# Turning the attention weights on TensorE in fp32, in the bank of their scores, and a list schedule for the issue order

## The chip, the core and the metric

The kernel runs on one core of a Trainium2 chip. The core has five instruction queues: PE (TensorE, matrix products), DVE (VectorE), ACT (ScalarE), POOL (GpSimd) and SP (SyncE, which only issues transfers here). ACT issues transfers as well. Each queue works strictly in its own order and waits for others by semaphores. The metric is the time of one execution in microseconds (us).

## The reference, cut to what matters

```python
# q, k, v: 4 batches x 8 heads x 576 tokens x 64, float32
scores = scale * q @ k.T                       # 576 x 576 for each of 32 heads
thresh = max(scores, -1) - tau
scores = where(scores >= thresh, scores, -1e9)
attn = exp(scores - max); attn = attn / (sum(attn) + 1e-9)
x = attn @ v                                   # put together: 2304 tokens x 512
# two blocks of products on x
h = ((x @ w1) * (x @ w2)) @ w3 @ w_out
out = elu(h @ w_in) @ w_out2
```

## The kernel before

The program has an attention phase and then products in sequence. Only the phase is changed.

**Tiles.** The 32 heads go as 16 pairs. The scores of a pair are cut into 9 tiles of 128 queries by 576 keys, 144 tiles in all. The tiles of the first four pairs (NPL = 4, 36 tiles) multiply queries and keys in plain fp32 and are called plain tiles here. The others use queries and keys that were split into a high and a low part in fp32r. A tile passes through these steps, each an operation of its own:

- `emit_S` (PE, L367 for plain tiles, L379 for the others) writes the scores into `s`, which takes two banks of PSUM. There are three such buffers, so six of the eight banks.
- `emit_max` (DVE, L388) takes the row maximum into `st`. `emit_tiny` (DVE, L392) makes the threshold and the bias of the exponential from it.
- `emit_exp` (ACT, L396) writes `e` in SBUF. `emit_mask` (DVE, L402) sets what lies under the threshold to zero and sums the rows. This is the last reader of `s`.
- `emit_H` (ACT, L409) rounds `e` to fp16 and `emit_L` (POOL, L413 and L414) makes the fp16 rest. Both lie in `hl`.
- `emit_T` (SP, L424, L426, L429) turns `hl` by a transposing transfer into `pt`, the keys on the partitions.

A group is a pair's first four or last five tiles, 256 or 320 tokens. `emit_PV` (PE, L483) multiplies a group's `pt` with the values `v` in fp16, as three partial products (high by high, low by high, high by low): 28 matmuls into 64 rows each. The values were scaled and split before that (`v_sum`, `v_mean`, `v_scale`, `prep_v`, `prep_vl`: ACT, PE, DVE). Row sums go another way: `turn_r` (PE, L443) transposes the 4 or 5 columns of reciprocals, and a store and a load spread them over partitions (`rd`, `rb`). `emit_xf` (DVE, L491) multiplies the two, and `emit_xh`, `emit_xl` split the result into `x`.

**First layers.** `emit_ab` (PE, L525) computes a = x w1 and b = x w2. One unit is 12 matmuls over four pairs of one batch, 256 or 320 tokens wide. The units of three of the four batches belong to the phase and fill PE between tiles; they need the batch's x and the converted weights. `pv`, `ab` and a small filler product (`keep_busy`, L384, during the first 18 tiles) share the two banks that are left.

**Order.** The phase's operations are written down with what each needs, and a table of letters says in which order they are issued. Each queue then holds its instructions in this order. Behind the phase come the last batch's first layers, M = w3 w_out (L828), x2 = g M (L968) and the second layers (L1001, L1030).

Of the kernel before, what the change touches and what calls it, by code (L numbers as in the profile page):

```python
# [7 lines left out]
F32 = mybir.dt.float32  # L8
# [35 lines left out]
PSCALE = 2.0 ** 14
VSCALE = 2.0 ** 15
LNS = 14 * 0.6931471805599453
KINDS = dict(
    a="emit_H",
    b="emit_L",
    c="emit_PV",  # L50
    d="emit_S",
    e="emit_T",
    f="emit_exp",
    g="emit_mask",
    h="emit_max",
    i="emit_rr",
    j="emit_tiny",
    k="emit_xf",
    l="emit_xh",
    m="emit_xl",  # L60
    n="evict_a",
    o="evict_g",
    p="high",
    q="join",
    r="keep_busy",
    s="keep_r",
    t="load_plain",
    u="load_qk",
    v="load_r",
    w="load_v",  # L70
    x="load_w",
    y="low",
    z="prep_h",
    A="prep_lk",
    B="prep_lq",
    C="prep_v",
    D="prep_vl",
    E="rest",
    F="run_ab",
    G="sign",  # L80
    H="store_g",
    I="store_r",
    J="top",
    K="turn_r",
    L="v_mean",
    M="v_scale",
    N="v_sum",
)
# the order in which the operations of the attention phase are issued
ORDER = (  # L90
    "wttdNxwdwhjdfhjgfthtdjgfhadgJbLjhdftEearjMfgbahdCtgbaxjGdeNbhaihfeKrbjjLqrfrerfwggedauDbspxhdMajgyfI",
    "hdCijgrfbrhJdegajEdeNbhaKGLsrfbejrhacqfIbgpegdayMJjDdhNvrifjbheagfbjekdfglxEKLershavdgbaGdCuhbacjjMq",
    "fbfgephdgJIyjhdfmaigKeabhdCjjDsefbhavcgefbDaIdezEbjgfkAdaxhgbejhdafGBejifvgKcbqeaslhbpdekglxmjehdfyk",
    "ajgfhdabmljgrfhbzdgJwjmhdBiaejEKFahfIbeGFfugbjegfdqaAedsngavbhpxdhbacjjhfoyfIjgfegdzkbidhJgrAajhdfeE",
    "blKFjageaGbdsnhfveqcbaNugebpjhdfIkFmehajBjgfxFofgydJgdhndaeizbLhFjjEavbeFhfMaobgefcGabjgnelfqKdbaHFh",
    "seCuBgdpIkdjhmFfiyjofegKFlgsJdhbndDavIobcejhahabfeEFjkfwmgHzvAFeGgnabdjofFqabhdpcjgbfehnaugydeNFkjhf",
    "eidajbgKFslhfImoedlgzLFbjehnfvdjBoeFfMgaAhHCdiHcgnbavhaujbmefDdKgFAejkfwhbdajgaFbhesfojaIgdbenrfhdaF",
    "BjgfhzbudgeFaijbhfvejoKNdgbFsahenfBjLdMHgcfbehaIoeabjdgfFhezAijkfvdgAFnugChbeldoaKrjhsdbefjDaFmgeahl",
    "bfdcnIhBzvgjjbfdeawFgmavkbhfudiFjagbelofhdNAeFjgnfhbHadoezKLjcBMgCehsbfDdeaFkwgbHahedniBFajhfjbfIgKF",
    "ujgmfoedAsndglaembFhazvhbejdjofcbgfuIhaAgdejhdfvBiagNvbhdajeKLcsbMfIjkehabljgfekdabgfehdavbgezidhbre",  # L100
    "ajrhrfbjjKsvgcfumfBgeldkmdgelahmdaIehbFCjjhabeDfFjfgwbngfdcAzvgeoaihadbeNudhFjbhefkajgKBFesfjfgbednL",
    "aIdheFabMglCoHbdjhHfFiajgAenfvmKdhFbegsaIjhfbdeoaDFzjgwnhBfvdocuhbajjgfAagdefFkbagzvdhbdNuhFenibajhf",
    "ejjKLFsBfgIeofgAdnczgehbaiejdkbfFheljauMmgdfvbFoahCgbeadDKndajbhefchsvAejjgffgbdHFzkHgBelhadFawjbhfi",
    "jobdfIgFuheaBgnKdjoselbFhNIfeLAdMngFavejmadfuboFheahCbcgzvjibnjDfdekFfBgvHhadmgFabjlheaKdjsofwbecfgb",
    "nIgezhAdjFehfkadjHofvbFggNdehncailjhbfuemajdkKFgbsaehfdboaeLjFgfhmlIedjabMFgnCeiBdzvoFDfhmKawFAjgfen",
    "dbsvochuaAjeghadbHkfjFlgbefhdzIgFbejnhfdBjoFfgahmudegFabnjhNdboeaFihfjbavHjgKLFsnefbfgdeAcaoaHgbzehd",
    "FMbekjifhBdaIjgFnlhfBejCKdgbFsvmeofhadgeabFnIhujjAfvdofcDbggzvdehFkahaubjdlFfhmniawejbKfFogbejadfchB",
    "HngzebjgdfeFkNgseahIdbLFhelajjMfbodfgFAaignedhbFjoHfeBagdavheAKFahnsjmjHfdbFgobfIhdnvcgbChvjDfdejiaw",
    "ckhbagfKjFksfgeagdlNFemhobjdenlLFaMbhfIejdobFgeihdneaFhfbjmKHfFgsvogHdCFehnaIjjfdbveoaFhbDecnjavgfbf",
    "gFekldFoagHbdcnaeabdeFkibldKeFosImeFmneFovHdFncvoFkldFmnoH",  # L110
)
# [48 lines left out]
def attention_moe_moe2(  # L160
# [56 lines left out]
    def conv_ops(key, parts, eng):  # L217
        """Steps that turn a loaded chunk into the parts (x -> (high, low)) it is used in."""
# [43 lines left out]
    mul2 = cst.tile([P, 2], F32, name="mul2")  # L262
# [14 lines left out]
    def load_plain(p, j, eng=A):  # L277
# [221 lines left out]
    def xl_pool(p, n):  # L499
        return int(n == 1 or p % 2)  # L500
# [610 lines left out]
```

## Time and profile before

| | us |
|---|---|
| time, three runs | 1074.71 (median), 1073.62, 1080.15 |
| span of the profiled execution | 1067.1 |
| median less span | 7.6 |
| PE busy | 970.9 (91%) |
| DVE busy | 644.9 (60%) |
| ACT busy | 519.7 (49%) |
| POOL busy | 484.5 (45%) |

The profile shows one execution; its own time is not listed apart, so its span is set against the median, and 7.6 us are taken as what lies around the span. Start times count from the span's start. PEld is TensorE's weight load, which runs beside PE. A merged row of the timeline gives the start of the first instruction, the time covered and the count; the length of a matmul is that of one alone, longer than the step from one to the next.

### The profile page before, as it was taken

To read this page: it belongs to the slowest core of one execution; us is meant where nothing else is said; L and a number is where in the kernel's file an instruction comes from. 1 tells how busy PE (TensorE), PEld (TensorE's weight loads), DVE (VectorE), ACT (ScalarE), POOL (GpSimd) and SP (SyncE) were. 2 spreads that over 40 slices of the span, in tenths; PEclk is the share of its full clock that TensorE was granted. 3 is DMA by queue.
4 is the path that set the end of the run, shared out by engine and by line. 5 is a ranking of instruction groups with operands and counts; after the bars stand their busy time and mean duration, and the time that the engine had idled before them with its cause. 6 is when DMAs were issued, how large, how long until landed. Compare 5 with 4: busy or idle time off the path is not lost.

```text
span 1067.1 us, 16849 instructions
## 1 busy us (share of the span) xinstructions
PE 970.9 (91%) x6132; PEld 871.6 (82%) x6132; DVE 644.9 (60%) x1200; ACT 519.7 (49%) x870; POOL 484.5 (45%) x494
## 2 busy tenths in 40 slices
PE   7476788878888798889999999999999999999998
PEld 4344677777888788789879999989999999999997
DVE  7799999867888698636564664943332232323322
ACT  5566776756776675525344565433233232322322
POOL 3568888877777675614221232232222222222221
PEclk9879999988999899999999999999999999999999
DMA  8989999999999999977616673300000000000000
GB/s 236 162 176 224 187 182 186 194 180 156 207 208 183 183 161 161 156 184 240 219 58 220 204 243 114 119 1 30 1 1 30 1 30 1 1 30 1 31 1 29
DMA packets 207342, 131.52 MB, mean 123 GB/s; under 512 B 175792, under 2 KB 194460, under 8 KB 202652
## 3 DMA queue, kind: packets, MB, share of 16 engines
q1 hardware_dynamic: 189520, 66.45, 39.1%
q10 hardware_dynamic: 17740, 64.01, 20.2%
q8 instruction: 48, 0.79, 0.3%
q14 instruction: 34, 0.28, 0.1%
HBM read 73.73 MB, written 14.23 MB: 82 GB/s over the span
## 4 chain that ended last, share of the span: by engine, by line
PE 62%; DMA 16%; DVE 15%; ACT 2%; issue 2%; POOL 1%; SPq 1%; ACTq 0%; POOLq 0%; DVEq 0%
PE h L1001 18%; PE o L1030 18%; PE x L968 10%; PE ab L525 9%; DMA pt<-hl 8%; DMA rb<-rd 4%; DVE e L402 4%; PE m L828 4%; DVE st L388 3%; DVE st L392 3%; DMA rqk<-in_qk 2%; PE s L379 1%; PE s L367 1%; DMA rd<-rt 1%; ACT e L396 1%
## 5 line engine op out<-in xcount | busy, mean ns | idle before, releaser
L525 PE MATMUL ab<-x,W 128*128 128x256 f32 (+1 forms) x1536 | 222.2, 299 | 9.7 <-DVE xf L491 5.8
L525 PEld LDWEIGHTS ab<-x,W 128*128 128x128 f32 x1536 | 209.8, 191 | 13.5 <-DVE xf L491 4.5
L413 POOL TENSOR_TENSOR hl<-e,hl 128x512 f16<-128x512 f32 x144 | 171.7, 1192 | 104.3 <-ACT hl L409 90.7
L1001 PE MATMUL h<-sl,W 128*128 128x384 f32 x1152 | 216.5, 336 | 0.0
L1030 PE MATMUL o<-WO,sl 128*128 128x512 f32 x864 | 213.8, 392 | 0.8 <-POOL sl L1022 0.8
L1001 PEld LDWEIGHTS h<-sl,W 128*128 128x128 f32 x1152 | 203.7, 188 | 7.7
L1022 POOL TENSOR_TENSOR sl<-th,sl 128x384 fp32r<-128x384 f32 x87 | 88.1, 1013 | 265.7 <-ACT sl L1017 265.7
L1030 PEld LDWEIGHTS o<-WO,sl 128*128 128x128 f32 x864 | 160.9, 188 | 29.4 <-POOL sl L1022 1.2
L1010 DVE TENSOR_SCALAR th<-h 128x384 f32<-128x384 f32 x96 | 53.4, 556 | 182.1 <-PE h L1001 182.1
L396 ACT ACTIVATE e<-s,st,esc 128x576 f32<-128x576 f32 x144 | 117.5, 826 | 72.8 <-DVE st L392 57.5
L1011 ACT ACTIVATE th<-th 128x384 f32<-128x384 f32 x96 | 50.4, 525 | 193.7 <-DVE th L1010 193.7
L402 DVE SCALAR_TENSOR_TENSOR e<-s,st,e 128x576 f32<-128x576 f32 x144 | 115.3, 807 | 18.9 <-ACT e L396 18.4
L379 PE MATMUL s<-qk 128*128 128x288 f32 x480 | 91.1, 320 | 32.4 <-DVE e L402 27.2
L409 ACT ACTIVATE hl<-e 128x576 f16<-128x576 f32 x144 | 94.8, 674 | 35.4 <-DMA pt<-hl 23.1
L388 DVE TENSOR_REDUCE st<-s 128x1 f32<-128x576 f32 x144 | 106.9, 747 | 8.0 <-PE s L379 4.6
L379 PEld LDWEIGHTS s<-qk 128*128 128x128 f32 x480 | 72.8, 201 | 43.2 <-issue 19.4
L968 PE MATMUL x<-sl,M 128*128 128x384 f32 x576 | 101.9, 338 | 0.0
L968 PEld LDWEIGHTS x<-sl,M 128*128 128x128 f32 x576 | 101.5, 187 | 0.3 <-DVE sl L215 0.2
L1015 DVE SCALAR_TENSOR_TENSOR th<-th,h 128x384 f32<-128x384 f32 x96 | 53.2, 554 | 58.2 <-ACT th L1011 57.4
L1017 ACT ACTIVATE sl<-th 128x384 fp32r<-128x384 f32 x96 | 50.3, 524 | 76.9 <-PE o L1030 47.6
L483 PE MATMUL pv<-pt,v 128*64 128x256 f16 (+1 forms) x896 | 66.3, 300 | 13.1 <-DMA pt<-hl 8.2
L392 DVE SCALAR_TENSOR_TENSOR st<-mul,st,add 128x2 f32<-128x2 f32 x144 | 76.5, 541 | 0.8
(86 smaller groups left out, 1033.9 us busy)
## 6 DMA issues: line engine op xcount, KB each, us to landing
rqk<-in_qk ACTq DMA_DIRECT2D x24, 576.0 KB
raw_wo<-in_wo ACTq DMA_DIRECT2D x12, 1024.0 KB
th<-g_dr SPq DMA_DIRECT2D x48, 192.0 KB
raw_w<-in_w ACTq DMA_DIRECT2D x8, 1024.0 KB
raw_w<-in_w3t ACTq DMA_DIRECT2D x8, 1024.0 KB
raw_win<-in_win ACTq DMA_DIRECT2D x8, 1024.0 KB
g_dr<-g SPq DMA_DIRECT2D x16, 320.0 KB
out<-r SPq DMA_DIRECT2D x18, 256.0 KB
```

The costliest lines, as they stand in the source:

```text
L379: T.matmul(s[:, n, :HS], q, k[:, c:c + HS], start=(x == 0), stop=(x == len(ops) - 1))
L388: V.tensor_reduce(st[i][:, 0:1], sc[i][:, :, :HS], axis=AX.XY, op=ALU.max, negate=True)
L392: V.scalar_tensor_tensor(t[:, 1:3], mul2, t[:, 0:1], add2, op0=ALU.mult, op1=ALU.add)
L396: A.activation(et[i], sc[i][:, :, :HS], AF.Exp, bias=st[i][:, 2:3], scale=esc)
L402: V.scalar_tensor_tensor(et[i], sc[i][:, :, :HS], st[i][:, 1:2], et[i], op0=ALU.is_ge, op1=ALU.mult, accum_out=sm[p][:, pos:pos + 1],)
L409: A.activation(hl[i][:, :S], et[i].rearrange("p a b -> p (a b)"), AF.Copy)
L413: G.tensor_tensor(t[:, S + 64:], e[:, :512], t[:, :512], op=ALU.subtract)
L525: T.matmul(o[:, :w], wf[:, m, wx, kt, :], x[:, xx, :], start=(k == 0), stop=(k == 3 * NK - 1))
L968: T.matmul(o[:, :TB], M[:, f, mx, e * P:(e + 1) * P], gh[j, f][:, gx, :], start=(k == 0), stop=(k == 23),)
L1001: T.matmul(o[:, :TB], WI[f][:, wx, kt, :], xh[j, kt][:, xx, :], start=(k == 0), stop=(k == 3 * NK - 1),)
L1022: (V if jobs else G).tensor_tensor(x[:, 1, :], thin[2 + f % 2], f32(x[:, 0, :]), op=ALU.subtract)
L1030: T.matmul(po[j, t], gg[j, f][:, gx, t * P:(t + 1) * P], WO[f // 2][:, f % 2, wx, :], start=(f == 0 and k == 0), stop=(f == NF2 - 1 and k ...
```

## The change

1. The weights of a tile are no longer split and turned by transfer. `emit_X` transposes `e` on PE in five blocks of 128 keys, in fp32, into the banks that held the tile's scores (the fourth and fifth block overlap by 64 keys, and the values of that half block are zero). `emit_C` (ACT) copies the 640 columns to `pt`, now fp32. So a tile's `s` is held until `emit_C` is done. `emit_H`, `emit_L` and `emit_T` are gone.
2. `emit_PV` multiplies `pt` with the values as they are, in fp32: ten matmuls of 64 rows in place of 28, issued as five pieces. The five steps that scaled and split the values are gone.
3. The threshold is made on POOL (`emit_tiny`); the bias of the exponential is the maximum itself, since the queries are scaled once on POOL (`prep_s`); plain tiles make it on POOL (`emit_bias`). `emit_xl` is on POOL always.
4. The loads and stores of the phase that ACT issued are issued by SP.
5. The letter table is replaced by a list schedule that runs while the program is written. Each operation has an engine, a length and a key; at each step the engine that can start first takes, among the operations ready within 0.05 us, the one with the lowest key. Units of `ab` are cut into pieces of three matmuls. A tile's transposes have its number less 2 as key.
6. Buffers: `e` 5 in place of 4, values 4 in place of 1.

```diff
-            SP.dma_start_transpose(pt[g][:, :, j, c:c + P], hl[i])
+    def emit_X(i):
+        e = et[i].rearrange("p a b -> p (a b)")
+        o = sc[i].rearrange("p a b -> p (a b)")
+        for c in range(5):
+            k = min(c * P, S - P)
+            T.transpose(o[:, c * P:(c + 1) * P], e[:, k:k + P], ident)
+
+    def emit_C(i):
...
+        x = sc[i].rearrange("p a b -> p (a b)")[:, :5 * P].rearrange("p (c q) -> p c q", c=5)
...
+            A.activation(pt[g][:, :, j, c:c + P], x, AF.Copy)
-    def emit_PV(p, n):
+    def emit_PV(p, n, c):
...
+        for j in range(2):
+            x_ = q[:, c, j, :w // D if p < NPL else w]
+            T.matmul(
+                po_[p, n][j * D:(j + 1) * D, :w], vt[p][:, j, c * D:(c + 1) * D], x_,
+                start=(c == 0), stop=(c == 4),
+            )
-        V.scalar_tensor_tensor(t[:, 1:3], mul2, t[:, 0:1], add2, op0=ALU.mult, op1=ALU.add)
+        G.tensor_scalar(t[:, 1:2], t[:, 0:1], -1.0, add2[:, (k := int(i >= NPL * TPP)):k + 1], op0=ALU.mult, op1=ALU.add)
-    "wttdNxwdwhjdfhjgfthtdjgfhadgJbLjhdftEearjMfgbahdCtgbaxjGdeNbhaihfeKrbjjLqrfrerfwggedauDbspxhdMajgyfI",
+                t, o = min(((t, o) for t, o in cand if t <= t0 + 0.05), key=lambda x: (x[1].key, place[id(x[1])]))
-        ring["s", i] += [mx, ex, mk]
+        xo = op(call(emit_X, i), [mk], "PE", 0.5, i - 2)
+        co = CC[i] = op(call(emit_C, i), [xo], "ACT", 0.68, i - 3)
+        ring["s", i] += [mx, ex, mk, xo, co]
```

PE's queue around tile 105 in the kernel before (the number behind s or e is the tile; the last number only names the buffer):

```order
L379 MATMUL s105_3953<-qk11_1288 128x288 x4
L525 MATMUL ab1_0_1_1_3962<-x4_0_1782,W1_468 128x256 x3
L525 MATMUL ab1_0_1_1_3962<-x5_0_2296,W1_468 128x256 x3
L525 MATMUL ab1_0_1_1_3962<-x6_0_2639,W1_468 128x256 x3
L525 MATMUL ab1_0_1_1_3962<-x7_0_2938,W1_468 128x256 x3
L379 MATMUL s106_3985<-qk11_1288 128x288 x4
L525 MATMUL ab1_0_2_0_3992<-x4_0_1782,W2_623 128x256 x3
L525 MATMUL ab1_0_2_0_3992<-x5_0_2296,W2_623 128x256 x3
L525 MATMUL ab1_0_2_0_3992<-x6_0_2639,W2_623 128x256 x3
L525 MATMUL ab1_0_2_0_3992<-x7_0_2938,W2_623 128x256 x3
L443 MATMUL s105_3953<-ident_115,rr11_0_3942 4x128
L379 MATMUL s107_4018<-qk10_1071 128x288 x2
```

Here scores and units of `ab` alternate, and a tile stands once in the queue. PE's queue around tile 108 in the changed kernel (L329 scores, L370 transposes, L475 `ab`, L400 `turn_r`):

```order
L329 MATMUL s108_3842<-qk8_740 128x288 x4
L475 MATMUL ab1_0_4_1_3850<-x4_0_1505,W4_723 128x256 x3
L475 MATMUL ab1_0_4_1_3850<-x5_0_1816,W4_723 128x256 x3
L475 MATMUL ab1_0_4_1_3850<-x6_0_2055,W4_723 128x256 x3
L475 MATMUL ab1_0_4_1_3850<-x7_0_2554,W4_723 128x256 x3
L329 MATMUL s109_3869<-qk8_740 128x288 x4
L400 MATMUL s109_3869<-ident_108,rr11_1_3830 5x128
L475 MATMUL ab1_0_5_0_3883<-x4_0_1505,W5_881 128x256 x3
L475 MATMUL ab1_0_5_0_3883<-x5_0_1816,W5_881 128x256 x3
L475 MATMUL ab1_0_5_0_3883<-x6_0_2055,W5_881 128x256 x3
L370 MATMUL s108_3842<-ident_108,e108_3867 128x128 x5
L475 MATMUL ab1_0_5_0_3883<-x7_0_2554,W5_881 128x256 x3
```

A tile now stands twice, with its transposes (which wait for its mask on DVE) ahead of the `ab` piece that needs nothing of it.

PE's queue around tiles 62 to 67 in the changed kernel, behind 16 units of `ab` in a row (64 pieces of 320 columns):

```order
L475 MATMUL ab0_1_7_1_2345<-x3_1_1415,W7_1180 128x320 x3
L370 MATMUL s62_2045<-ident_108,e62_2084 128x128 x5
L370 MATMUL s63_2064<-ident_108,e63_2094 128x128 x5
L370 MATMUL s64_2069<-ident_108,e64_2108 128x128 x5
L400 MATMUL s64_2069<-ident_108,rr6_1_2130 5x128
L329 MATMUL s65_2381<-qk11_1227 128x288 x4
L329 MATMUL s66_2388<-qk11_1227 128x288 x4
L438 MATMUL pv6_1_2398<-pt6_1_1974,vr6_1235 64x320 x2
L329 MATMUL s67_2406<-qk10_1080 128x288 x4
L438 MATMUL pv6_1_2398<-pt6_1_1974,vr6_1235 64x320 x6
L370 MATMUL s65_2381<-ident_108,e65_2404 128x128 x5
L438 MATMUL pv6_1_2398<-pt6_1_1974,vr6_1235 64x320 x2
```

In the kernel before a tile's scores stand between these units; now the scores of tiles 62 to 64 are ahead of the run and their transposes behind it, and no `ab` is left for the tiles that follow.

POOL's queue around tile 108 in the changed kernel (L342 the threshold, L283 and L287 the low parts of queries and keys, L266 the scaling):

```order
L287 TENSOR_TENSOR qk10_1080<-rqk26_3503,qk10_1080 128x576
L342 TENSOR_SCALAR st108_3855<-st108_3855,add2_107 128x1
L283 TENSOR_TENSOR qk11_1227<-rqk27_3587,qk11_1227 64x576
L287 TENSOR_TENSOR qk11_1227<-rqk27_3587,qk11_1227 128x576
L342 TENSOR_SCALAR st109_3894<-st109_3894,add2_107 128x1
L342 TENSOR_SCALAR st110_3924<-st110_3924,add2_107 128x1
L266 TENSOR_SCALAR rqk28_3878<-rqk28_3878,esc_105 128x576
L342 TENSOR_SCALAR st111_3959<-st111_3959,add2_107 128x1
```

The threshold of a tile, which was DVE's own, now stands behind the splitting of other heads' queries and keys.

## Rows read from the trace of the kernel before

**Rows 1.** The page: 40 slices (busy tenths), and the chain that ended last

```profile
PE   7476788878888798889999999999999999999998
...
PE 62%; DMA 16%; DVE 15%; ACT 2%; issue 2%; POOL 1%; SPq 1%; ACTq 0%; POOLq 0%; DVEq 0%
```

**Rows 2.** Windows: PE, PEld, DVE, ACT, POOL busy; PE clock, DMA share, GB/s

```profile
0.00:117.00 117.00, 79.38 (x571) 50.54 (x571) 101.87 (x201) 73.14 (x112) 75.11 (x87) 0.90 1.00 197
117.00:467.00 350.00, 296.19 (x2396) 270.91 (x2397) 280.24 (x613) 225.70 (x379) 251.86 (x293) 0.96 1.09 177
467.00:1067.10 600.10, 595.30 (x3167) 550.11 (x3165) 262.80 (x387) 220.86 (x380) 157.49 (x115) 1.00 0.23 77
```

**Rows 3.** Timeline of all engines at the end of the attention phase

```profile
462.87 3.00 PE L525 MATMUL ab<-x,W 128*128 128x256 f32 x24
...
466.46 8.77 PE L525 MATMUL ab<-x,W 128*128 128x320 f32 x58 [0.59 <-DVE g L540]
```

**Rows 4.** Waits from 0 to 467 us: total us, times, longest

```profile
ACT e L396 <- DVE st L392: 57.5, 56, 3.6
...
ACT hl L409 <- DMA pt<-hl: 23.1, 12, 7.6
...
PE pv L483 <- DMA pt<-hl: 8.2, 3, 6.0
```

**Rows 5.** Groups by form: busy us, mean ns; idle before and its releaser

```profile
L396 ACT ACTIVATE e<-s,st,esc 128x576 f32<-128x576 f32 x144 | 117.5, 826 | 72.8 <-DVE st L392 57.5 <-DVE vst L334 4.1 <-PE ab L525 3.6
L402 DVE SCALAR_TENSOR_TENSOR e<-s,st,e 128x576 f32<-128x576 f32 x144 | 115.3, 807 | 18.9 <-ACT e L396 18.4 <-POOL qk L305 0.2
L388 DVE TENSOR_REDUCE st<-s 128x1 f32<-128x576 f32 x144 | 106.9, 747 | 8.0 <-PE s L379 4.6 <-PE s L367 2.4 <-PE s L330 0.9
...
L409 ACT ACTIVATE hl<-e 128x576 f16<-128x576 f32 x144 | 94.8, 674 | 35.4 <-DMA pt<-hl 23.1 <-DVE e L402 7.0 <-DVE xf L491 2.5
...
L392 DVE SCALAR_TENSOR_TENSOR st<-mul,st,add 128x2 f32<-128x2 f32 x144 | 76.5, 541 | 0.8
...
L837 ACT ACTIVATE M<-m 128x512 fp32r<-128x512 f32 x8 | 4.7, 587 | 11.2 <-PE m L828 11.2
```

**Rows 6.** Timeline at 35 us: weight loads of the fp32 128x128 filler

```profile
35.64 0.97 PEld L384 LDWEIGHTS k<-spread 128*128 128x128 f32 x8
```

**Rows 7.** Timeline of PE, 0 to 117 us: start, length, form, count

```profile
5.92 7.23 PE L367 MATMUL s<-qkp 128*64 128x288 f32 x32 [1.94 <-DMA qkp<-in_qk]
...
94.64 2.98 PE L525 MATMUL ab<-x,W 128*128 128x256 f32 x24
...
107.43 2.16 PE L367 MATMUL s<-qkp 128*64 128x288 f32 x16 [1.12 <-DVE e L402]
...
110.30 1.19 PE L367 MATMUL s<-qkp 128*64 128x288 f32 x8
...
111.45 1.62 PE L525 MATMUL ab<-x,W 128*128 128x256 f32 x12
```

**Rows 8.** Timeline of PE, 230 to 300 us

```profile
247.96 2.09 PE L483 MATMUL pv<-pt,v 128*64 128x320 f16 x28
249.98 1.86 PE L379 MATMUL s<-qk 128*128 128x288 f32 x12
...
291.57 1.72 PE L483 MATMUL pv<-pt,v 128*64 128x256 f16 x28
293.22 0.80 PE L379 MATMUL s<-qk 128*128 128x288 f32 x4
```

**Rows 9.** Timeline at 314 us: a transpose in fp32, and the scores behind it

```profile
314.71 0.27 PE L443 MATMUL s<-ident,rr 128*5 128x128 f32 x1
...
314.73 0.78 PE L379 MATMUL s<-qk 128*128 128x288 f32 x4
```

**Rows 10.** Windows of 20 us: columns as in Rows 2

```profile
40.00:60.00 20.00, 12.12 (x75) 8.18 (x77) 13.65 (x25) 12.23 (x20) 11.37 (x12) 0.68 1.12 207
...
80.00:100.00 20.00, 12.38 (x106) 8.09 (x106) 19.19 (x37) 12.32 (x19) 16.56 (x18) 1.00 1.14 225
```

More of the change, by code (lines that the diff above doesn't have):

```diff
@@ L37 @@
 WARM = 6
+EB, PTB, VB = 5, 2, 4
 NKB = 18
 XB = (8, 6)
-ALPHA = dict(PE=2.3, DVE=2.3, ACT=2.3, POOL=2.3, SP=2.3)
-C0, CG, CS, CL, EV, LP, HLB = 2.0, 5.5, 1.0, 4.0, 0.5, 4.0, 5
-LQ, HQ, VK, RK = (-13.0, -8.0), (-8.0, -4.0), (-3.0, -0.5, 3, 1.5), (1.2, 3, 4.0)
+C0, CG = 2.0, 5.5
 FA, FB, FC = (24.0, 44.0), (20.0, 36.0), (8.0, 36.0)
[L44 to L88, printed above, removed]
@@ L138, in take, with hold @@
         return r[-1]
+    def hold(self, tag, n, first, last):
+        self.slots.setdefault(tag, (n, []))
+        first.gets, last.frees = tag, (tag, first)
     def turns(self):
@@ L478, in emit_PV @@
             q = q.rearrange("p c j t -> p c (j t)").rearrange("p c (t j d) -> p c j t d", j=2, d=D)
[L479 to L486 removed]
+        if c == 0:
+            po_[p, n] = ps_m.tile([P, 512], F32, tag="m", name=f"pv{p}_{n}")
+        for j in range(2):
[4 more added lines that the diff above has]
+            )
     def emit_xf(p, n):
@@ L588, in attention_moe_moe2 @@
             continue
-        mx = MAX[i] = op(call(emit_max, i), [o])
+        mx = MAX[i] = op(call(emit_max, i), [o], "DVE", 0.68, i)
         rs = take("st", 6, mx)
         if i < NKB:
-            box = []
-            box.append(op(call(keep_busy, i), [o]))
-        ty = op(call(emit_tiny, i), [mx])
-        ex = op(call(emit_exp, i), [ty])
-        re = take("e", 4, ex)
-        mk = MASK[i] = op(call(emit_mask, i), [ex])
+            kb = op(call(keep_busy, i), [o], "PE", 0.25, i + 500)
+            pl.hold("m", 2, kb, kb)
+        plain = p < NPL
+        bi = op(call(emit_bias, i), [mx], "POOL", 0.15, i - 10) if plain else mx
+        ty = op(call(emit_tiny, i), [mx, bi], "POOL", 0.15, i - 10)
+        ex = op(call(emit_exp, i), [bi], "ACT", 0.80, i)
+        re = take("e", EB, ex)
+        mk = MASK[i] = op(call(emit_mask, i), [ex, ty], "DVE", 0.75, i - 2)
         if pos == 0:
@@ L770, in attention_moe_moe2 @@
         else:
-            ev = op(call(evict_g, b, n, f, out_), [un, last["a"][0]])
+            ev = op(call(evict_g, b, n, f, out_), [un, last["a"][0]], "DVE", (0.36, 0.42)[n], key - 10)
             last["a"].append(ev)
```

363 lines of the change are left out of this document (153 added, 210 removed).

## The prediction

> **What bounds the kernel now.** I read the page's slices first. From the 18th slice on PE is busy in every tenth, before that in six to eight [rows 1]. The windows put numbers on it: 79.4 of 117 us, 296.2 of 350 us, then 595.3 of 600 us [rows 2]. The border is at 466.5 us, where the last batch's 320-column first layers start [rows 3]. Behind it PE sets the pace, and neither code nor data there change, so I leave those 600 us as they are. The question is only whether the attention phase, 466.5 us, gets shorter.
>
> In the phase no single engine is full. DVE is busy 101.9 + 280.2 = 382 us [rows 2]; 76.5 of them are `emit_tiny`, 541 ns each for two numbers a row [rows 5]. The exponentials waited 57.5 us for it, ACT 23.1 us and the group products 8.2 us for the turning transfers [rows 4]. The 16 transfer engines are loaded beyond one transfer each, 1.00 and 1.09 [rows 2], and on the chain transfers have 16%, DVE 15% [rows 1]. So the change removes what the tiles wait for: two DVE items and all turning transfers. But it pays on PE, and PE has 467 - 376 = 91 us free. That sum decides.
>
> **PE's work, step by step.** I price the back-to-back step of each form, not the length of one, since a length overlaps the next.
> - Plain scores: two tiles take 2.16 us and one 1.19 [rows 7], so 0.97 each, 36 tiles: 35 us. Other scores: (1.86 - 0.80) / 8 = 0.133 us a matmul [rows 8], 480 of them: 64 us.
> - `ab`: (2.98 - 1.62) / 12 = 0.113 us at 256 columns [rows 7]; at 320 columns 58 take 8.77 us [rows 3], 0.149 without the tail of the last. 576 of each in the phase: 65 + 86 = 151 us.
> - Group products before: from the first matmul to the scores behind it 1.65 us (256 columns) and 2.02 us (320) [rows 8]; 16 of each: 59 us. Filler 8 us; `turn_r`, `v_mean` and small ones about 10.
>
> That is 327 us of dense work in a phase of 466.5; 140 us are waits, tails and half clock.
>
> Added: **transposes.** 144 x 5 = 720, none of this shape in the trace. Lower bound: the fp32 `turn_r` matmul streams the same 128 columns, and the scores behind it start 0.02 us later [rows 9]; by that five cost 0.1 us. Upper bound: two passes, as the fp32 filler has. Nearest row: a block needs a 128x128 fp32 weight load of its own, and eight such loads take 0.97 us [rows 6], 0.115 each with the tail taken off. I take that: 0.575 us a tile, 83 us in all; ends 15 and 166.
>
> The Trainium skill ("TensorE: Matmul & The Clock Gate", Part 4: PE-mode transpose) gives about 275 ns for a 128x128 transpose inside a kernel; an estimate from that figure is 198 us for all, and a time of about 1190, to which I give no chance. The trace has 0.27 us for `turn_r` too [rows 9], but as the length of one, and the next product starts before it ends, so I don't add such lengths.
>
> **Group products in fp32.** The form closest is a plain tile: fp32, 64 rows, eight records of 288 columns in 0.97 us [rows 7]. A group has 20 records: 20 x 0.121 x 256/288 = 2.16 us, and 2.70 at 320 columns; 16 of each: 78 us. Cut into pieces they are entered 70 times from products 128 columns wide (counted in PE's new order). Leaving such a product costs extra: `ab` starts 1.15 us after a plain tile did, not 0.97 [rows 7]. At 0.15 that is 10 us. Against 59 before, +29. `v_mean` goes: -5.
>
> Sum: 83 + 29 - 5 = +107, so 434 us of dense PE work, and PE starts 6 us in [rows 7]: 440. **27 us are left for every wait of the phase.**
>
> **The other engines** have room, priced from [rows 5]. DVE loses `emit_tiny` and about 28 us of value and `xl` work: 382 - 105 = 277 us. ACT swaps a 674 ns rounding for a copy of 640 columns; the 512-column eviction took 587 ns, so about 0.70, +4 us, and loses value work and the issuing of transfers, which lands on SP, behind which only other transfers stand. POOL loses `emit_L`; its thresholds have no row, I take 0.2 us, but they queue behind the low parts of queries and keys, and a mask waits for its threshold. A late threshold delays the mask, then the transposes, then all that PE has behind them; before, DVE made it in place. That is the wait the change adds.
>
> **What waits remain.** (a) The first 16 tiles have no `ab` beside them, and `s` is held longer, by transposes and copy: about 6 us a tile over three buffers, 2 us, against 2.4 us of DVE and PE work a tile. I take 8 us lost. (b) The run of 16 units before the transposes of tiles 62 to 64 is no loss by itself, but tiles 65 to 73 then have no filler: 6. (c) From a tile's scores to its transposes maximum, exponential and mask take 0.75 + 0.83 + 0.89, with hand-overs about 3 us. In the new order PE has 3.0 us of other work there for tile 108 (seven pieces of three, the next scores, a `turn_r`), and counted likewise a median of 3.8 for tiles 72 to 143, with a quarter under 2.9. I take 0.1 us a tile: 7. (d) The end, where the last group's product and x stand alone: 4. (e) Half clock: before, the mean clock of the phase was 0.90 and 0.96 [rows 2], some 26 us lost; a denser PE should keep it up, 5. Together 30.
>
> So 440 + 30 = 470 against 466.5: +3. Span 1070, with 7.6 around it **1077 us**, no change. A measurement of this kernel tells about 1% (11 us) from none.
>
> **Rivals.**
> - *PE stalls on its own order (slower).* The list schedule puts transposes where its lengths say that they are ready; its mask has 0.75 us, the trace 0.81 + 0.08 [rows 5], and two tiles share DVE. If tiles from 36 on lose 0.35 us each in place of (c), 108 x 0.35 = 38, +31: about 1108. For: a quarter of the tiles has less than 2.9 us, and POOL may hold a threshold for two splits. Against: DVE is at 59%, and PE's own lengths in the schedule are no longer than mine. It decides from about 0.17 us a tile.
> - *Cheaper transposes (faster).* If the weight load of a transpose hides, a block costs its columns: 128 x 0.113/256 = 0.056 us, 40 us for all, -43. Then DVE and the banks cut in, and I give back 11: about 1045. For: `turn_r` lets the next product start at once. Against: there the load was 5 columns.
> - *The clock falls.* In the trace it stood at 0.68 where PE was busy 12.1 of 20 us, but at 1.00 where it was 12.4 of 20 [rows 10], so busy time alone does not tell. If transposes gave the gate no activity, the first 36 tiles (about 100 us of PE work, 20 of it transposes) would look like those windows, with a mean of 0.9 as now, and the tiles without `ab` worse: +15, about 1092. The same part of the same page of the Trainium skill says that a transpose does not count as busy for the clock; no run here shows it, since the 32 transposes before are single.
>
> **How the numbers follow.** Forecast 0.42 (1065 to 1092), stalls 0.25, cheaper transposes 0.25, clock 0.08. Faster by over 1% is the third and a little of the first: 0.29. Slower is the stalls, half of the clock case and the top of the forecast: 0.36. Within 1%: 0.35. The range goes from the cheap transposes to the stalls, 1045 to 1110.
>
> **What the new profile would show.** The 720 transposes start 0.11 to 0.12 us apart; PE is busy over 90% from the second window on; DVE is at about 277 us in the phase; the first L475 at 320 columns of the last batch starts at 470 us. PE's longest waits should be transposes for a mask. A transpose step of 0.06 or of 0.2 us, or a clock under 0.95 after 120 us, would make the prediction wrong, and so would masks that wait for POOL by the microsecond.

## The result and the profile after

The changed kernel takes 1088.33 us (median of four runs, 1087.62 to 1090.06) against 1075.54 for the kernel before in the same comparison (1073.62 to 1080.15). The ratio is 1.012, with a 95% interval from 1.009 to 1.016: slower by a little over 1%, and 11.3 us above the forecast of 1077, inside its range.

The page of the changed kernel: its 40 slices and the shares of the chain that ended last, to be set beside [rows 1].

```profile
PE   7989999999999999999999999999999999999998
...
PEclk9999999999999999999999999999999999999999
...
PE 90%; DVE 3%; DMA 2%; ACT 2%; issue 2%; SPq 1%; POOL 0%; DVEq 0%; ACTq 0%
```

PE is full from the fourth slice on; before it was the nineteenth (the 18th, which the prediction names, shows an 8). On the chain DVE falls from 15% to 3% and transfers from 16% to 2%. So the edits do what they say, and PE has become the bound of nearly the whole program. The clock row has a 9 in every slice; before, it had a 7 and four 8:

```profile
PEclk9879999988999899999999999999999999999999
```

Windows of the changed kernel, columns as in [rows 2] (PE, PEld, DVE, ACT, POOL busy, PE clock, DMA share, GB/s):

```profile
0.00:117.00 117.00, 103.68 (x746) 66.99 (x748) 85.26 (x161) 74.72 (x106) 65.17 (x105) 0.99 0.46 146
117.00:475.00 358.00, 350.67 (x2596) 296.21 (x2592) 207.21 (x448) 202.96 (x334) 122.56 (x197) 1.00 0.23 70
475.00:1085.80 610.80, 604.64 (x3225) 554.58 (x3224) 262.13 (x390) 222.13 (x383) 158.79 (x116) 1.00 0.23 77
```

PE's idle time is 13.3 us in the first window (37.6 before) and 7.3 us in the second (53.8 before, [rows 2]). The DMA share falls from 1.0 to 0.46 and from 1.09 to 0.23. The end of the attention phase in PE's timeline, which answers to [rows 3]:

```profile
480.15 3.11 PE L475 MATMUL ab<-x,W 128*128 128x256 f32 x24 [0.57 <-DVE g L490]
483.84 2.32 PE L475 MATMUL ab<-x,W 128*128 128x320 f32 x14 [0.59 <-DVE g L490]
```

The last batch's 320-column units start at 483.84 us, where the forecast had 470 and the kernel before 466.46. Behind them lie 602.0 us, before 600.6. So the loss is made in the phase: +17.4 of the span's 18.7 us. The median of the times rose by less, 12.8 us, because the profiled execution of before (span 1067.1) was a short one for that kernel: every run on record lies 1.8 us above its own span, so it took about 1069, and later single runs of that kernel lie between 1060 and 1096.

The phase as one window, the kernel before and then the changed one:

```profile
0.00:466.46 466.46, 375.03 (x2965) 320.91 (x2965) 382.11 (x813) 298.84 (x490) 326.97 (x379) 0.94 1.07 182
```

```profile
0.00:483.84 483.84, 462.03 (x3396) 368.94 (x3396) 293.71 (x611) 278.92 (x442) 188.61 (x303) 1.00 0.28 88
```

PE's idle time falls by 69.6 us (91.4 to 21.8), and its busy time rises by 87.0. That is the whole change of 17.4 us. DVE's busy time falls by 88 us, and nobody is faster for it, since PE has no gaps left in which to use it.

What PE's steps cost is read from its timeline in the changed kernel, start, length and count of a run of equal products. The step is the difference of two starts over the count.

```profile
26.90 2.38 PE L438 MATMUL pv<-pt,vr 128*64 128x256 f32 x20
29.21 0.71 PE L334 MATMUL k<-spread 128*128 128x128 f32 x4
...
194.81 24.36 PE L475 MATMUL ab<-x,W 128*128 128x320 f32 x165
219.01 1.80 PE L370 MATMUL s<-ident,e 128*128 128x128 f32 x15
220.65 0.27 PE L400 MATMUL s<-ident,rr 128*5 128x128 f32 x1
220.67 1.29 PE L329 MATMUL s<-qk 128*128 128x288 f32 x8
221.90 0.76 PE L438 MATMUL pv<-pt,vr 128*64 128x320 f32 x4
...
231.32 0.77 PE L370 MATMUL s<-ident,e 128*128 128x128 f32 x5
232.01 0.65 PE L438 MATMUL pv<-pt,vr 128*64 128x256 f32 x4
232.60 0.77 PE L370 MATMUL s<-ident,e 128*128 128x128 f32 x5
...
265.55 1.05 PE L475 MATMUL ab<-x,W 128*128 128x320 f32 x6
266.44 0.71 PE L370 MATMUL s<-ident,e 128*128 128x128 f32 x5
266.90 1.13 PE L475 MATMUL ab<-x,W 128*128 128x320 f32 x6
267.87 0.70 PE L329 MATMUL s<-qk 128*128 128x288 f32 x4
268.40 0.60 PE L475 MATMUL ab<-x,W 128*128 128x320 f32 x3
268.83 0.71 PE L370 MATMUL s<-ident,e 128*128 128x128 f32 x5
```

Fifteen transposes take 1.64 us, 0.109 each. A group of 256 tokens takes 2.31 us. The `ab` matmuls of 320 columns are 0.147 apart in the long run. Where kinds follow one another, some borders cost nothing. From 265.55 to 268.83 us stand fifteen `ab`, four scores (0.53 us, as forecast) and five transposes. Their steps add up to 2.21 + 0.53 + 0.55 = 3.28 us, and 3.28 us is what they take, with four changes of kind among them: the `ab` behind the transposes start 0.09 us early and take 0.09 us longer. Other borders do cost. From 231.32 to 232.60 us five transposes and four records of a group product take 1.28 us. Their steps are 0.55 + 0.43 (the 20 records of a group start in pairs, 0.216 us from pair to pair), so 0.30 us go to two borders, 0.15 each. Group products write 64 output rows; the others here write 128.

With these steps the phase adds up as follows. Dense is the count of each kind times its step. Idle is from the two windows. Half clock is what the stretches at 1.2 GHz took beyond the same work at 2.4. Between products is the rest, and forecast is the prediction's own sum. The column before is the short execution.

| us of the phase | before | after | forecast |
|---|---|---|---|
| dense products | 318.6 | 419.5 | 424 |
| between products | 31 | 41 | 10 |
| half clock | 26 | 2 | 5 |
| PE idle | 91 | 22 | 31 |
| sum | 467 | 484 | 470 |

An estimate, fitted to the starts of all of PE's records in the phase outside the half clock, says where the 41 us lie: 153 borders of group products come to 0.15 us each, some 24 us, and the 114 borders between transposes and `ab` to nothing within 0.03.

### The profile page after: what moved, and what is told of

Read it like the earlier page. It is cut to its first block, busy times and chain, and to the rows that moved or that the text cites. A ratio compares the mean times of both kernels' runs of the same rounds, so it can differ in the third digit from the quotient of the medians.

```text
span 1085.8 us, 16950 instructions
## 1 busy us (share of the span) xinstructions
PE 1059.0 (98%) x6564; PEld 917.8 (85%) x6564; DVE 554.6 (51%) x998; ACT 499.8 (46%) x822; POOL 346.5 (32%) x418
## 4 chain that ended last, share of the span: by engine, by line
PE 90%; DVE 3%; DMA 2%; ACT 2%; issue 2%; SPq 1%; POOL 0%; DVEq 0%; ACTq 0%
PE h L916 18%; PE o L945 18%; PE ab L475 18%; PE x L883 9%; PE pv L438 8%; PE s L370 7%; PE s L329 5%; PE m L743 4%; PE s L317 2%; DVE e L359 1%; DMA rb<-rd 1%; DMA rqk<-in_qk 1%; DVE st L338 1%; DVE rr L394 1%; ACT e L353 0%
## 5 line engine op out<-in xcount | busy, mean ns | idle before, releaser
L475 PE MATMUL ab<-x,W 128*128 128x256 f32 (+1 forms) x1536 | 234.2, 301 | 1.2 <-DVE g L490 1.2
L475 PEld LDWEIGHTS ab<-x,W 128*128 128x128 f32 x1536 | 209.6, 188 | 12.1 <-issue 6.9
L370 PE MATMUL s<-ident,e 128*128 128x128 f32 x720 | 105.4, 279 | 5.9 <-DVE e L359 5.5
L370 PEld LDWEIGHTS s<-ident,e 128*128 128x128 f32 x720 | 80.1, 141 | 32.4 <-DVE e L359 17.9
L342 POOL TENSOR_SCALAR st<-st,add 128x1 f32<-128x1 f32 x144 | 43.2, 300 | 172.5 <-DVE st L338 171.9
L438 PE MATMUL pv<-pt,vr 128*64 128x256 f32 (+1 forms) x640 | 94.2, 417 | 0.8 <-DVE g L490 0.8
L353 ACT ACTIVATE e<-s,st 128x576 f32<-128x576 f32 x108 | 78.5, 736 | 32.2 <-DVE st L338 31.7
L386 ACT ACTIVATE pt<-s 128x640 f32<-128x640 f32 x96 | 67.2, 702 | 54.3 <-PE s L370 54.1
L329 PE MATMUL s<-qk 128*128 128x288 f32 x480 | 83.8, 302 | 0.7 <-ACT pt L386 0.6
```

The source lines that it names most:

```text
L329: T.matmul(s[:, n, :HS], q, k[:, c:c + HS], start=(x == 0), stop=(x == len(ops) - 1))
L353: A.activation(et[i], sc[i][:, :, :HS], AF.Exp, bias=st[i][:, 0:1])
L370: T.transpose(o[:, c * P:(c + 1) * P], e[:, k:k + P], ident)
L386: A.activation(pt[g][:, :, j, c:c + P], x, AF.Copy)
L438: T.matmul(po_[p, n][j * D:(j + 1) * D, :w], vt[p][:, j, c * D:(c + 1) * D], x_, start=(c == 0), stop=(c == 4),)
L475: T.matmul(o[:, :w], wf[:, m, wx, kt, :], x[:, xx, :], start=(kt == 0 and k == 0), stop=(kt == NK - 1 and k == 2),)
```

## The experiments

All times are medians. Single runs of the kernel before range from 1060 to 1096, those of one variant by 0.7% or less, so a variant of the changed kernel is set against that kernel's 1088.3. The changed kernel was not run again beside its variants. The kernel before was, with medians from 1072.9 to 1075.5, so a difference of 3 us between variants is not sure. The table gives the time, the ratio to the kernel before with its interval, the end of the phase (the start of the last batch's 320-column units), PE's idle time up to there (end less the busy time of that window) and the mean clock of the first 117 us.

| kernel | time | ratio | phase | PE idle | clock to 117 |
|---|---|---|---|---|---|
| changed | 1088.3 | 1.012 [1.009, 1.016] | 483.8 | 21.8 | 0.99 |
| x_two | 1065.2 | 0.995 [0.992, 0.999] | 464.1 | 37.6 | 0.94 |
| x_two_late | 1071.8 | 0.996 [0.994, 0.999] | 468.7 | 24.2 | 0.97 |
| x_two_early | 1083.2 | 1.010 [1.006, 1.013] | 477.3 | 28.4 | 0.97 |
| x_half | 1092.1 | 1.021 [1.012, 1.029] | 488.5 | 21.5 | 0.96 |
| tiny_dve | 1087.4 | 1.016 [1.010, 1.023] | 484.0 | 22.2 | 0.99 |
| old_tiny_pool | 1087.8 | 1.016 [1.008, 1.023] | 484.8 | 106.4 | 0.85 |
| pv_whole | 1093.0 | 1.022 [1.015, 1.029] | 488.6 | 32.5 | 0.97 |
| pv_wide | 1111.3 | 1.036 [1.031, 1.040] | 511.0 | 21.0 | 0.97 |
| ab_whole | 1090.9 | 1.020 [1.011, 1.028] | 485.6 | 23.2 | 0.99 |
| no_filler | 1091.3 | 1.017 [1.013, 1.021] | 487.5 | 28.3 | 0.94 |
| true_lengths | 1102.1 | 1.029 [1.022, 1.036] | 498.8 | 33.1 | 0.94 |
| lengths_whole | 1099.4 | 1.027 [1.020, 1.034] | 495.6 | 31.8 | 0.96 |

### Fewer transposes: x_two, x_two_late, x_two_early

Two of a tile's five transposes are left, in all tiles, in the tiles from 72 on, and in the tiles below 72. The rest of the weights is left out, so these three do not compute the reference.

```diff
-        for c in range(5):
+        for c in (2, 3):                                  # x_two
+        for c in ((2, 3) if i >= 72 else range(5)):       # x_two_late
+        for c in ((2, 3) if i < 72 else range(5)):        # x_two_early
```

> Only two of a tile's five transposes are issued (the copy reads old scores for the rest, so the output is not the reference's). Theory A, the phase lasts as long as PE's dense work: 144 x 3 blocks at the 0.109 us step seen in the changed kernel are 47 us, and the time falls by 40 to 47 us, to about 1044. Theory B, the phase is set by waits of the new order (a tile's chain from scores to copy, masks that wait for POOL): the chain loses 0.33 us a tile but PE only waits longer, and less than 25 us come back, above 1063.

> Three of five transposes are left out for tiles 72 to 143 alone (the output is not the reference's). There PE has next to no idle time in the changed kernel. Theory A (where PE has no gap, time follows its dense work one to one; where tiles have no filler, the tile chain sets it): 72 x 3 x 0.109 = 23.5 us come back, about 1065, nearly all that leaving them out everywhere gave. Theory C (the loss in leaving them out everywhere was spread over all tiles): about half of those 23 us, 1076.

> The same three transposes left out for tiles 0 to 71 alone (the output is not the reference's). Theory A: the idle time of PE and the stretches at half clock grow by what is saved, so within 6 us of 1088. Theory C: about half of 23 us, 1076.

Taken out were 432 transposes, 47 us at 0.109, or 216, 23.5 us, in each half. The time fell by 23.1 us in all, 16.5 in the late half and 5.2 in the early half. The windows of x_two, to 117 us and to the end of its phase, show where the rest went:

```profile
0.00:117.00 117.00, 95.68 (x636) 55.74 (x636) 86.03 (x159) 73.32 (x104) 60.89 (x102) 0.94 0.47 145
117.00:464.10 347.10, 330.81 (x2332) 267.37 (x2328) 209.55 (x453) 202.62 (x338) 125.58 (x202) 1.00 0.24 73
```

PE's idle time rises from 13.3 to 21.3 us in the first window and from about 8.5 to 16.3 us in the second, and the clock of the first window falls from 0.99 to 0.94, which loses 6 us of 117. So in the first tiles the other engines stand close behind PE and take over when PE is relieved; in the later ones seven tenths of the saving arrive. Neither of the two pure pictures held: the late half gave 16.5 where a pure PE bound says 23.5, the early half 5.2, nearly nothing as PE-independent tiles would give. Even with three fifths of the transposes left out, the change wins only 0.5% over the kernel before.

### What a transpose's cost is: x_half

The fifth block becomes 64 keys wide, so its weight load has half the columns; the products with it run over 64 keys.

```diff
-        for c in range(5):
-            k = min(c * P, S - P)
-            T.transpose(o[:, c * P:(c + 1) * P], e[:, k:k + P], ident)
+        for c in range(4):
+            T.transpose(o[:, c * P:(c + 1) * P], e[:, c * P:(c + 1) * P], ident)
+        T.transpose(o[:D, 4 * P:5 * P], e[:, 4 * P:], ident)
...
+        K = D if c == 4 else P
...
-                po_[p, n][j * D:(j + 1) * D, :w], vt[p][:, j, c * D:(c + 1) * D], x_,
+                po_[p, n][j * D:(j + 1) * D, :w], vt[p][:K, j, c * D:(c + 1) * D], x_[:K],
...
```

> The fifth block has 64 keys in place of 128, with the values laid to match; the result is the same. Theory A: if a block costs its weight load, half a load is saved 144 times, 8 us, about 1080. If a 64-column block pays for a change of width as the group products do (0.09 us in and 0.09 out), it costs 18 us more, about 1106. Theory B: no change, 1088.

PE's timeline of x_half, three tiles' transposes in a row:

```profile
222.42 0.60 PE L369 MATMUL s<-ident,e 128*128 128x128 f32 x4
222.86 0.27 PE L370 MATMUL s<-ident,e 128*64 128x128 f32 x1
222.97 0.60 PE L369 MATMUL s<-ident,e 128*128 128x128 f32 x4
...
224.06 0.27 PE L400 MATMUL s<-ident,rr 128*5 128x128 f32 x1
```

The narrow block is followed 0.11 us later by the next (222.86 to 222.97), and all fifteen take 1.64 us, the same as with five full blocks. The mean length of its weight load is 111 ns against 141 for a full one. So the weight load does not set the step, and the 1080 us that half a load would have given did not come. What is left is the 128 columns that stream through. 0.109 us at 2.4 GHz is 2.04 cycles for a column, and a record of 256 columns into 128 rows takes twice that (0.216 us, pv_wide below); no run varies the columns of a transpose, so this half is argued. The kernel itself is 3.7 us slower than the changed one. The clock of the first window is 0.96 in place of 0.99, which is worth about 3.4 us; products over 64 keys now stand between those over 128 as well.

### The threshold on POOL: tiny_dve and old_tiny_pool

tiny_dve puts the threshold and the plain tiles' bias of the changed kernel back on DVE. old_tiny_pool puts both on POOL in the kernel before, two instructions for every tile.

```diff
-        G.tensor_scalar(t[:, 1:2], t[:, 0:1], -1.0, ...)
+        V.tensor_scalar(t[:, 1:2], t[:, 0:1], -1.0, ...)
...
-        G.tensor_scalar(t[:, 2:3], t[:, 0:1], esc, 0.0, op0=ALU.mult, op1=ALU.add)
+        V.tensor_scalar(t[:, 2:3], t[:, 0:1], esc, 0.0, op0=ALU.mult, op1=ALU.add)
```

```diff
-        V.scalar_tensor_tensor(t[:, 1:3], mul2, t[:, 0:1], add2, op0=ALU.mult, op1=ALU.add)
+        G.tensor_scalar(t[:, 2:3], t[:, 0:1], esc, LNS, op0=ALU.mult, op1=ALU.add)
+        G.tensor_scalar(t[:, 1:2], t[:, 0:1], -1.0, add2[:, 0:1], op0=ALU.mult, op1=ALU.add)
```

> The threshold and the plain tiles' bias go back from POOL to DVE, each 0.15 us there. Theory A: DVE has room and PE's work is the same, so within 4 us of 1088. Theory B, masks wait for POOL behind the splitting of queries and keys: 8 us or more come back, 1080 or less.

> The kernel before with one part of the change alone: threshold and bias of a tile are made on POOL by two instructions, not on DVE by one. Theory A (before, the phase was held by DVE's chain maximum, threshold, exponential, mask, with 57.5 us of exponentials waiting for the threshold): DVE loses 76 us, the exponentials start earlier, 8 to 25 us are won, 1050 to 1066 against 1075. Theory B (the turning transfers and POOL's own queue set the pace: a threshold stands behind low parts of 1 to 1.5 us on POOL): same or slower, 1075 to 1100.

In the changed kernel it makes no difference: 1087.4 and 1088.3, PE idle for 22.2 and 21.8 us. DVE does 35 us more work there and PE does not see it. In the kernel before the step costs 14 us (1087.8 against 1073.6, a ratio of 1.016, from 1.008 to 1.023). The first row of its waits on ACT in the phase (total us, times, longest):

```profile
ACT e L397 <- POOL st L392: 126.0, 87, 4.0
```

The exponentials waited 57.5 us for the threshold on DVE [rows 4]; now they wait 126.0 us for it on POOL. POOL has `emit_L` there, 1181 ns for one of its two pieces in this run, and is busy 407 of 485 us; a bias of 304 ns queues behind such pieces. Of the two theories, that DVE's relief wins 8 to 25 us failed, and that POOL's queue sets the pace (1075 to 1100) held. Two things differ in the changed kernel: POOL has no `emit_L`, and in the 108 tiles that are not plain the exponential takes the maximum itself and does not wait for POOL. The runs do not tell which of the two makes the step harmless there.

### Pieces and widths: pv_whole, ab_whole, pv_wide

pv_whole issues a group's ten products in one piece and not five; ab_whole issues the 12 matmuls of a unit in one and not four.

```diff
+    def whole_PV(p, n):
+        for c in range(5):
+            emit_PV(p, n, c)
...
-            pv = op(call(emit_PV, p, n, c), [pv], "PE", (0.44, 0.55)[n], q + 5)
+        pv = v0 = op(call(whole_PV, p, n), VV[p] + [CC[i] for i in tiles] + pvs[-1:], "PE", (2.2, 2.75)[n], q + 5)
```

```diff
+    def whole_ab(b, n, f, m, out_):
+        out_.append(emit_ab(b, n, f, m))
...
-            un = op(call(run_ab, b, n, f, m, out_, kt), [un], "PE", (0.35, 0.445)[n], key)
+        u0 = un = op(call(whole_ab, b, n, f, m, out_), need, "PE", (1.4, 1.78)[n], key)
```

> A group's product is issued as one operation, not as five pieces. Theory A, a change between 64 and 128 columns costs 0.09 us on each side: 70 entries become some 32, 38 x 0.19 = 7 us less, about 1081. Theory B: transposes now stand behind up to 2.7 us of product, and PE waits more where it has no filler: 1088 or more.

> Units of ab are issued whole (12 matmuls) in place of four pieces of three; the schedule may no longer put transposes or scores between the pieces. Theory A (changes of product width on PE are part of what the forecast missed, about 0.1 us each way, 180 of them): fewer changes, so PE's busy time falls by some us, but a transpose that becomes ready waits up to 1.8 us, tiles go round more slowly, and idle rises in the first third: 1083 to 1095. Theory B (the pieces cost nothing, and what they give is worth much): idle rises by over 15 us, 1100 or more.

The phases of both as one window, pv_whole and then ab_whole:

```profile
0.00:488.60 488.60, 456.11 (x3396) 376.13 (x3396) 289.07 (x611) 276.57 (x442) 187.50 (x303) 0.99 0.29 87
```

```profile
0.00:485.60 485.60, 462.41 (x3397) 371.50 (x3397) 294.13 (x611) 279.34 (x442) 186.01 (x303) 0.99 0.28 88
```

In pv_whole PE changes 110 times and not 180 times between products of 64 and of 128 output rows, and its busy time falls by 5.9 us, though the half clock took up to 5 us more of it: 0.085 to 0.16 for each change saved. But a transpose that becomes ready has to wait for a whole group, the tiles go round later, idle time rises by 10.7 us, and the kernel is 4.7 us slower. Counted by the scores in PE's timeline, tile 72 starts at 246.4 us and not at 234.7, and the phase behind it takes 242.2 us and not 249.1. So the one piece loses 12 us in the first half, a part of it by the clock, and wins 7 in the second. ab_whole lies inside what was expected of it: about 4 us less between products, given back to idle time and half clock.

pv_wide computes the groups of 256 tokens with values of both heads in one 128-wide product, of which half the output is used.

```diff
-            T.matmul(
-                po_[p, n][j * D:(j + 1) * D, :w], vt[p][:, j, c * D:(c + 1) * D], x_,
...
+            if n == 0:
+                o, v = po_[p, n][:, j * w:(j + 1) * w], vt[p][:, 2 * c_ * D:2 * (c_ + 1) * D]
```

> For the 256-token groups the values of both heads are loaded together, 128 columns wide, one head after the other into its own half of the bank (half of each product is not used), so that PE does not change between widths; DVE takes the product in two operations; the result is the same. Theory A: about 35 entries and exits at 0.19 us, less a dearer weight load, 4 to 6 us come back, about 1083. If the widths cost nothing by themselves: 1088 or more.

PE's timeline of pv_wide:

```profile
302.53 3.61 PE L443 MATMUL pv<-pt,vr 128*128 128x256 f32 x16
305.98 0.71 PE L370 MATMUL s<-ident,e 128*128 128x128 f32 x5
```

Sixteen records take 3.45 us, 0.216 each, where the records of 64 output rows take 2.31 / 20 = 0.116 with a part of the borders. So two products into 64 rows each take as long as one into 128. Getting rid of the width change by doubling the width therefore costs 28 us in PE's busy time (489.96 against 462.03 in the phase).

### The filler: no_filler

```diff
-NKB = 18
+NKB = 0
```

> The 18 filler products (72 matmul records, 10 us of PE in the first third) are left out; the result is the same. Theory A: they stand where the tile chain sets the pace, so at most 5 us come back, 1083 to 1088. Rival: the clock falls in the first 100 us without them and each stretch at half clock costs, 1090 to 1100.

Windows from 20 to 40 and 60 to 80 us, no_filler and then the changed kernel:

```profile
20.00:40.00 20.00, 15.00 (x86) 7.69 (x86) 12.53 (x26) 11.35 (x17) 9.11 (x17) 0.76 0.51 201
...
60.00:80.00 20.00, 15.99 (x110) 9.62 (x106) 14.96 (x31) 14.31 (x22) 14.78 (x23) 0.91 0.25 90
```

```profile
20.00:40.00 20.00, 17.26 (x116) 10.75 (x117) 13.35 (x27) 13.19 (x20) 11.71 (x18) 0.91 0.51 202
...
60.00:80.00 20.00, 15.98 (x123) 10.28 (x122) 15.58 (x31) 14.30 (x21) 13.45 (x21) 1.00 0.27 90
```

The filler is 8 us of work, and taking it out makes the kernel 3 us slower: the mean clock of 20 to 40 us is 0.76 and not 0.91, that of 60 to 80 us 0.91 and not 1.00. The mean clock of the whole run is 0.991 to 0.993 in all four runs, against 0.996 to 0.998 in the changed kernel's. So the rival that the clock falls (1090 to 1100) held; the 3 us themselves are no more than variants with edits elsewhere differ by.

### The schedule's lengths: true_lengths, lengths_whole

The list schedule is given the lengths that the trace of the changed kernel shows; lengths_whole also issues the groups from tile 72 on in one piece.

```diff
-LAT = 0.15
+LAT = 0.25
...
-        ex = op(call(emit_exp, i), [bi], "ACT", 0.80, i)
+        ex = op(call(emit_exp, i), [bi], "ACT", 0.83 if plain else 0.74, i)
...
-        mk = MASK[i] = op(call(emit_mask, i), [ex, ty], "DVE", 0.75, i - 2)
+        mk = MASK[i] = op(call(emit_mask, i), [ex, ty], "DVE", 0.9, i - 2)
...
-        xo = op(call(emit_X, i), [mk], "PE", 0.5, i - 2)
+        xo = op(call(emit_X, i), [mk], "PE", 0.55, i - 2)
...
+        if q >= 72:                                       # lengths_whole
+            pv = v0 = op(call(whole_PV, p, n), deps, "PE", (2.4, 2.9)[n], q + 5)
...
```

> The list schedule is given the lengths that the trace of the changed kernel shows (maximum 0.75, exponential 0.83 or 0.74, mask 0.90, copy 0.71, threshold 0.30, transposes 0.55 us, hand-over 0.25 us); nothing else is changed. Theory A (PE is full, and its own gaps are small: 19.4 us idle up to the last batch's first layers, most of it in the first 180 us, where the other engines set the pace): little is to be won, the time is 0 to 6 us less than the changed kernel's 1088, so 1082 to 1088. Theory B (the rival of the prediction, stalls because the schedule's lengths are too short): the gaps of PE go, and what is behind them with it; 12 to 20 us less, 1068 to 1076.

> The true lengths, and from tile 72 on the group products in one piece, where PE no longer waits for other engines. Theory A (the pieces cost some 6 us in changes of width, and one piece costs idle time only in the first third): 4 to 8 us less than the changed kernel, 1080 to 1084. Theory B (one piece delays transposes in the later tiles too): the same as with true lengths alone or up to 6 us more.

Both expectations of true_lengths failed: it is 13.8 us slower than the changed kernel. Its timeline, the rows about the longest gap of PE:

```profile
12.42 0.33 SPq L190 DMA_DIRECT2D raw_w<-in_w  x1
...
20.82 0.26 POOL L346 TENSOR_SCALAR st<-st,esc 128x1 f32<-128x1 f32 x1
...
23.29 1.12 ACT L205 ACTIVATE u_w<-raw_w 128x1024 f32<-128x1024 f32 x1 [7.04 <-DMA raw_w<-in_w]
...
24.31 1.54 ACT L351 ACTIVATE e<-s,st,esc 128x576 f32<-128x576 f32 x2
...
26.11 1.11 PE L370 MATMUL s<-ident,e 128*128 128x128 f32 x4 [8.48 <-DVE e L359]
```

The bias that an exponential needs is ready at 21.08 us. But ahead of the exponential ACT has the conversion of a weight, which waits 7.04 us for its load, until 23.29. The schedule gives such a load 6 us; this one was issued at 12.42, so it took 10.9. Mask and transposes come after it, and PE stands for 8.48 us; the changed kernel's longest gap there is 4.11. Behind it the clock is down, and it falls once more where the new order leaves tiles without `ab`:

```profile
200.00:220.00 20.00, 14.59 (x107) 11.20 (x107) 12.15 (x28) 11.15 (x17) 10.53 (x15) 0.90 0.38 101
220.00:240.00 20.00, 17.89 (x105) 12.39 (x104) 11.03 (x23) 11.41 (x18) 8.89 (x13) 0.84 0.25 59
```

In the changed kernel these two windows have a clock of 1.00. PE's idle time is 11.3 us more than there, and some 10 us more are lost to the half clock (0.94 to 117 us and 0.98 behind, against 0.99 and 1.00); about 6 us come back between products. Engine lengths closer to the trace made another order, and that order meets transfers whose arrival the schedule had wrong. lengths_whole is 2.7 us faster than true_lengths. Tile 72 starts at the same time in both (251.8 and 251.7 us), so the one piece helps late, where PE hardly waits, though less than the 4 to 8 us that I gave it; its own number, 1080 to 1084, failed with the base that it stands on. No variant beats both kernels with the whole computation.

## Why the prediction was right or wrong

**What bounds the phase.** Right in the main: the removed waits pay on PE, and PE's sum decides. In the tiles below 72 it does not decide alone: with 23.5 us of transposes left out there, 5.2 us were won (x_two_early). DVE's and the transfers' shares of the chain went from 15% and 16% to 3% and 2%, and DVE's 88 us came to nothing in themselves, as tiny_dve shows from the other side. DVE is busy for 294 us, not for 277, and that changed nothing either.

**Dense work.** Right within 5 us: 419.5 us against 424 without entries. Transposes step 0.109 us where I took 0.115; a group of 256 tokens takes 2.31 us up to the next product where I had 2.16 and its entry of 0.15.
- The rival of *cheaper transposes* falls: 0.109, not 0.056, and x_half shows why. With a smaller weight load the step stays 0.109 us, so it is not the load that the step shows; a transpose takes about two cycles for each of its columns, where the rival has one. The lower bound had rested on `turn_r`, behind which the next scores start at once [rows 9]. They do so after too (220.65 and 220.67 us), but from the first of those scores to the second it is 0.217 us, where a step is 0.131: the time stands behind the early start.
- The Trainium skill ("TensorE: Matmul & The Clock Gate", Part 4: PE-mode transpose) has about 275 ns for one, of bf16. The trace has 279 ns as the mean length of L370 and 0.109 as the step; so the estimate of 198 us from that figure does not hold for transposes in a row.

**Between products.** This is the term that was mis-sized. The prediction put 10 us, 70 entries into group products at 0.15, and let all other products stand edge to edge. It had read 140 us of the phase before as "waits, tails and half clock" and then carried none of the tails over into the new sum. By the table the term is 41 us, at 510 changes from one kind of product to another; before, it was 31 us at 290, counted in PE's timeline.
- A group product costs about 0.15 us when it is entered and again when it is left (231.32 to 232.60 us above; pv_whole has 0.085 to 0.16 for a change). The prediction charged one of the two sides. By the estimate above some 24 of the 41 us lie here.
- Borders among transposes, `ab` and the scores that are not plain cost next to nothing (265.55 to 268.83 us). Here "edge to edge" was right.
- The other 17 us, plain tiles and restarts behind waits among them, are not told apart.

Mis-sized by 31 us, this is the largest error, and it alone would have turned the forecast into 1108. Dense work was put 5 us too high, waits 9 and half clock 3, so 17 us came back. That the time lies only 11 us from the forecast is in part luck.

**What waits remain.** Too dear: 6 us at the start and 25 us of waits against 21.8 measured, 13.3 of them before 117 us (forecast 6 + 8) and 8.5 behind (forecast 17). PE's two longest waits in the changed kernel, 0 to 300 us (total us, times, longest):

```profile
PE s L370 <- DVE e L359: 5.5, 6, 1.9
PE s L317 <- ACT pt L381: 5.4, 5, 4.1
```

Transposes wait for a mask six times in 144, not 0.1 us a tile (c). So *PE stalls on its own order* is refuted for this order; true_lengths shows that the rival is a real one, since another order of the same operations loses 15 us in the phase, by gaps and the clock. Its cause was not the one that I named (a mask's length), but a queue behind a load.

**Half clock.** 2 us where I put 5. *The clock falls* is refuted: the granted clock is 0.99 to 117 us and 1.00 behind, with 720 transposes in the phase. That a transpose does not count as busy for the clock (the Trainium skill, the same page and part) shows nowhere here; but blocks of five to fifteen stand between products that are no transposes, so no run here tests it by itself. Before, the phase had lost 26 us to the lower level; that gain I had priced right.

**The threshold on POOL.** Named as the wait that the change adds; it adds none (tiny_dve), and masks do not wait for POOL. In the kernel before the step costs 14 us (old_tiny_pool). Whether the lost `emit_L` or the exponentials that no longer need POOL make the difference is open.

**Around the span.** The 7.6 us between span and median were spread from run to run, not a cost: each run is 1.8 us above its own span. So the forecast of the span, 1070, was 16 us too low, and 5 us of that were hidden in the time by this second error.

**What is not settled.** The half-clock stretches of the first 117 us differ between variants whose edits lie elsewhere (0.96 for x_half, 0.97 for pv_wide, 0.99 for tiny_dve) and are worth up to 3.5 us; what starts them was not found. Why the change between 64 and 128 output rows costs time is not shown either, only that it does. With one profile each, 3 us are not told apart from the edits.

## What to carry to other kernels

When work is moved onto the engine that becomes full, sum steps and then look in the trace of the kernel before for the borders between kinds that cost time, and charge both sides: here 0.15 us each time a product into 64 output rows is entered or left, and next to nothing between transposes and `ab`. A wait removed is worth only what the next engine has free: 70 us of PE's idle time were bought with 101 us of PE's work. Finer pieces and guessed lengths in a schedule were better here than their tidy versions, so such an order is timed, not argued.

## What was not expected of the hardware

Two fp32 products into 64 rows each, in the two halves of an output, cost about as much as one into 128 rows. At 256 columns their records start in pairs, 0.007 us apart, with 0.216 us from pair to pair, and a record into 128 rows steps 0.216 us too (pv_wide): the two of a pair run side by side. What this saves is paid in part at the borders, 0.15 us on each side. A transpose with a weight load of 64 columns steps 0.109 us, the same as with 128. And with 72 filler records of 0.112 us left out, PE had 8 us less to do, the clock was lower in all four runs, and the time was 3 us longer and not shorter.
